# Rounding the weights in place, lagging the activation, and leaving the order of the elementwise engines to the scheduler

## The chip, the cores and the metric

The kernel runs on one core of a Trainium2 chip. The metric is the device time of one launch in microseconds. TensorE multiplies matrices, VectorE, ScalarE and GpSimd do the elementwise work, SyncE issues DMAs. In the profile they are PE (PEld for its weight loads), DVE, ACT, POOL and SP.

## What is computed

A gated linear attention over 4 batches, 8 heads, 768 tokens and a head size of 48, then a feed-forward block on the 3072 tokens of width 384, with 2048 hidden units. The inputs `q`, `k`, `v` and the logits are float32. The weights come in as float64 words and are rounded to float32 on the chip.

```python
def _attn_ref(q, k, v, f_logit):
    f = 1.0 / (1.0 + np.exp(-f_logit))
    for t in range(S):
        state = f[:, :, t, :, None] * state + np.einsum('bhd,bhe->bhde', k[:, :, t], v[:, :, t])
        y[:, :, t] = np.einsum('bhd,bhde->bhe', q[:, :, t], state)

def _moe_ref(x, w_in, w_out):
    h = x @ w_in
    sp = np.maximum(h, 0.0) + np.log1p(np.exp(-np.abs(h)))
    g = h * erf(sp)
    return (g @ w_out).astype(np.float32)
```

## The kernel before

**Tiling.** The tokens are cut into 24 chunks of 128 (index `g`), three of which make one of 8 blocks of 384. A chunk of attention goes through four stages: `stage_d` (cumulated logits `ps_d` on TensorE, two exponentials `dp` and `dm` on ScalarE, `qd` on VectorE, `kd` on GpSimd, and a small DMA `Tall`), `stage_t` (transposes, copies `qT` and `kT`), `stage_s` (scores `sc`, masked to `A` on VectorE; the state's update `dS`, `Sn`, `Mbd`) and `stage_y` (the output `y`, copied to `xT`). `prepare` and `prepare_log` (L264 to L274) make the logarithm `lt` for a whole block.

**Feed-forward.** `hidden` makes one group of 4 of the 16 hidden tiles: 12 matmuls of 384 columns, each shown as two MATMUL records in the trace, into a pair of PSUM banks `hps`, of which there are two; after every 6 the copy of L426 moves a pair to the group's buffer `Hg`. There are seven such buffers. `activate` then works on a group of 128 x 1536: Exp and Ln on ScalarE, four squares `x` on ScalarE (L150) each multiplied into `e` on VectorE (L155), Tanh (L394), and the last multiply (L396). `project` multiplies all 16 tiles of a block by `w_out_sb` for each of three token tiles (L445), copies the result (L453) and stores it.

**Order.** Everything stands in one hand-written order for all engines (`tc.manual_schedule()`): each engine runs its instructions as the program lists them. The loop over `it` walks through slots, one slot a matmul of `hidden` or `project`. Pass it=0 has 48 slots (`hidden` of block 0); passes 1 to 6 have 96 (three groups of block `it`, the projection of block `it`-1, then the fourth group); it=7 is similar, with the fourth group inside the projection; it=8 has the last projection. Between slots stand the attention stages of the next block (`at`), an `act_step` at each odd slot, and `prepare` of block it+2 in the middle. `act_step` advances one group at a time, in nine steps. A chain of three chunks stands ahead of it=0.

**Weights.** They come in 16 pieces (8 of `w_in`, 8 of `w_out`), loaded as raw words into `Hg` buffers that are not yet in use (`raw_buf`), by `next_piece` on SyncE. `round_piece` takes Abs (L234, ScalarE), max (L235, GpSimd), four operations on VectorE (L239, L243, L246, L249), and an add (L254: VectorE for `w_in`, GpSimd for `w_out`). The intermediate tile `w_t` comes from the two buffers of tag "x", which the activation's `x` uses too. `weights_step` ends the piece before and begins the next. A piece ends before the next load into its buffer, and `hidden` uses a buffer only after its last piece.

## Time and profile before

| what | us |
|---|---|
| median of 3 runs (lowest, highest) | 879.63 (877.65, 879.96) |
| the profiled execution: its time | 878.28 |
| its span, first to last instruction | 876.6 |
| TensorE, matmuls busy | 684.9 |
| ScalarE busy | 533.3 |
| VectorE busy | 504.7 |
| GpSimd busy | 146.5 |
| mean granted TensorE clock, as a share | 0.903 |

The page gives busy shares of each engine; the list of waits says which instruction an engine stood idle for; the timeline shows instructions in order of time with the idle time before each and what ended it. A table by stage sums the busy time in stretches of the span. A line number is that of the kernel before.

### The profile page before, as it was taken

What the parts mean: (1) busy time and instruction counts of PE and PEld (TensorE: products, weight loads), DVE (VectorE), ACT (ScalarE), POOL (GpSimd) and SP (SyncE); (2) the same over time, 40 slices, a digit from 0 to 9 for tenths busy, and PEclk for the clock granted to TensorE, in tenths of its full rate; (3) what the DMA queues carried; (4) which work ended last, traced back from release to release, by engine and by line L of the source; (5) the groups of instructions that cost most, each with busy time, mean ns of one, the idle gap of its engine ahead of it and who ended that gap; (6) DMA issues with size and microseconds to landing.
All of it is one profiled execution on the core that took longest, in us unless ns stands there. A gap on an engine that the chain in (4) does not pass through costs nothing.

```text
span 876.6 us, 9159 instructions
## 1 busy us (share of the span) xinstructions
PE 684.9 (78%) x3729; PEld 410.2 (47%) x3729; DVE 504.7 (58%) x429; ACT 533.3 (61%) x457; POOL 146.5 (17%) x95
## 2 busy tenths in 40 slices
PE   3756636376888987978698886978698879989696
PEld 2524423244555554644455553644455545545353
DVE  3968775577562884277552884266552875185440
ACT  5264634277975779178745779178744776389450
POOL 2433445501210130000310130000310010000000
PEclk9868868779899899999899998999899999989999
DMA  9913145200113001400033001400030000000000
GB/s 222 261 49 93 45 105 147 35 1 0 37 37 63 1 1 37 99 0 1 1 73 63 1 1 37 99 0 1 1 73 10 1 0 19 10 1 0 18 10 30
DMA packets 112176, 36.88 MB, mean 42 GB/s; under 512 B 103936, under 2 KB 107008, under 8 KB 112128
## 3 DMA queue, kind: packets, MB, share of 16 engines
q1 hardware_dynamic: 108672, 36.18, 17.2%
q8 instruction: 31, 0.51, 0.2%
q10 hardware_dynamic: 3456, 0.05, 0.2%
q14 instruction: 17, 0.14, 0.1%
HBM read 31.46 MB, written 4.72 MB: 41 GB/s over the span
## 4 chain that ended last, share of the span: by engine, by line
ACT 29%; DVE 26%; PE 26%; issue 12%; POOL 4%; DMA 1%; ACTq 0%; SPq 0%; DVEq 0%; POOLq 0%
DVE e L155 17%; PE ops L445 15%; PE hps L419 7%; ACT x L150 5%; ACT yl L381 4%; ACT e L379 4%; ACT L381 3%; ACT e L394 3%; POOL w_out_sb L254 2%; ACT dp L285 2%; ACT L285 1%; PE y L144 1%; DVE Hg L426 1%; POOL w_t L235 1%; DVE qd L293 1%
## 5 line engine op out<-in xcount | busy, mean ns | idle before, releaser
L419 PE MATMUL hps<-xT,w_in_sb 128*128 128x384 f32 x768 | 290.9, 531 | 71.5 <-DVE Hg L426 65.1
L155 DVE SCALAR_TENSOR_TENSOR e<-x,e 128x1536 f32<-128x1536 f32 x128 | 244.2, 1908 | 109.7 <-ACT x L150 103.6
L445 PE MATMUL ops<-w_out_sb,Hg 128*128 128x384 f32 x768 | 274.0, 512 | 0.6 <-ACT osb L453 0.6
L419 PEld LDWEIGHTS hps<-xT,w_in_sb 128*128 128x128 f32 x768 | 154.4, 207 | 189.4 <-DVE Hg L426 71.8
L150 ACT ACTIVATE x<-yl,serf_bias 128x1536 f32<-128x1536 f32 x128 | 199.4, 1573 | 62.6 <-DVE e L155 44.3
L445 PEld LDWEIGHTS ops<-w_out_sb,Hg 128*128 128x128 f32 x768 | 151.6, 201 | 106.1 <-issue 19.5
L426 DVE COPY Hg<-hps 128x768 f32<-128x768 f32 x64 | 60.8, 951 | 94.5 <-PE hps L419 94.3
L298 POOL TENSOR_TENSOR kd<-kn,dm 128x384 f32<-128x384 f32 x24 | 32.6, 1360 | 421.6 <-ACT dm L289 257.2
L379 ACT ACTIVATE e<-Hg 128x1536 f32<-128x1536 f32 x32 | 47.2, 1475 | 63.9 <-DVE Hg L426 62.7
L394 ACT ACTIVATE e<-e 128x1536 f32<-128x1536 f32 x32 | 47.4, 1483 | 54.8 <-DVE e L155 53.8
L396 DVE TENSOR_TENSOR Hg<-Hg,e 128x1536 f32<-128x1536 f32 x32 | 62.3, 1946 | 22.0 <-ACT e L394 21.9
L293 DVE TENSOR_TENSOR qd<-qn,dp 128x384 f32<-128x384 f32 x24 | 20.6, 859 | 87.9 <-ACT dp L285 87.4
L279 PE MATMUL ps_d<-lt,tri 128*128 128x384 f32 x48 | 25.4, 617 | 40.0 <-ACT lt L274 40.0
L311 PE MATMUL ps_t<-ident,kd 128*128 128x128 f32 x96 | 19.4, 339 | 42.0 <-DVE Sn L356 38.9
L144 PE MATMUL y<-A,vt 128*32 128x128 f32 x768 | 39.0, 295 | 16.4 <-DVE kT L316 15.1
L381 ACT ACTIVATE yl<-e 128x1536 f32<-128x1536 f32 x32 | 47.5, 1483 | 0.4
L359 POOL TENSOR_TENSOR Mbd<-Sn,Tall 48x192 f32<-48x192 f32 x32 | 30.3, 947 | 99.7 <-DVE Sn L356 98.5
L144 PEld LDWEIGHTS y<-A,vt 128*32 128x32 f32 x768 | 29.4, 115 | 29.7 <-DVE kT L316 17.1
L235 POOL TENSOR_SCALAR w_t<-w_t 128x768 f32<-128x768 f32 x16 | 37.3, 2332 | 26.8 <-ACT w_t L234 26.7
L381 ACT ACT_TABLE_LOAD x32 | 41.1, 1283 | 0.6
L370 ACT COPY xT<-y 128x384 f32<-128x384 f32 x24 | 11.3, 471 | 43.8 <-PE y L144 43.8
L234 ACT ACTIVATE w_t<-Hg 128x768 f32<-128x768 f32 x16 | 14.3, 903 | 35.9 <-POOL w_out_sb L254 28.6
(53 smaller groups left out, 496.2 us busy)
## 6 DMA issues: line engine op xcount, KB each, us to landing
Hg<-in_moe_w_in_dram SPq DMA_DIRECT2D x8, 768.0 KB, 6.7
Hg<-in_moe_w_out_dram SPq DMA_DIRECT2D x8, 768.0 KB, 4.4
lt<-in_f_logit_dram SPq DMA_DIRECT2D x24, 192.0 KB, 3.6
qn<-in_q_dram SPq DMA_DIRECT2D x24, 192.0 KB, 3.6
kn<-in_k_dram SPq DMA_DIRECT2D x24, 192.0 KB, 3.8
vt<-in_v_dram SPq DMA_DIRECT2D x24, 192.0 KB, 3.8
out_dram<-osb SPq DMA_DIRECT2D x24, 192.0 KB, 2.0
Tall<-dp ACTq DMA_DIRECT2D x24, 2.0 KB, 2.0
```

What stands on the lines that cost most here:

```text
L144: nc.tensor.matmul(y[M * i : M * (i + 1), kt, :], lhsT=terms[n][0], rhs=terms[n][1], start=(n == 0), stop=(n == len(terms) - 1), skip_grou ...
L150: nc.scalar.activation(out=dst[:], in_=y[:], func=AF.Square, bias=serf_bias[:, i : i + 1], scale=SERF_K)
L155: nc.vector.scalar_tensor_tensor(out=e[:], in0=x[:], scalar=SERF_AB[i][1], in1=e[:], op0=ALU.add, op1=ALU.mult)
L235: nc.gpsimd.tensor_scalar(out=x.bitcast(FP32), in0=x.bitcast(FP32), scalar1=TINY, scalar2=None, op0=ALU.max)
L298: nc.gpsimd.tensor_tensor(out=kds[g % 2][:, :, 0:D], in0=kns[g % NQ][:].rearrange("t (h d) -> t h d", d=D), in1=dm[:].rearrange("t (h d) - ...
L379: nc.scalar.activation(out=e[:], in_=h, func=AF.Exp)
L381: nc.scalar.activation(out=y[:], in_=e[:], func=AF.Ln, scale=SERF_C, bias=1.0)
L394: nc.scalar.activation(out=e[:], in_=e[:], func=AF.Tanh)
L396: nc.vector.tensor_tensor(out=h, in0=h, in1=e[:], op=ALU.mult)
L419: nc.tensor.matmul(hps[:, j, 0:TB], lhsT=w_in_sb[:, kt, ft * P : (ft + 1) * P], rhs=xTs[blk][:, kt, :], start=(kt == 0), stop=(kt == n_k - 1),
L426: nc.vector.tensor_copy(out=gr["h"][:, 2 * u : 2 * u + 2, :], in_=hps[:, :, 0:TB])
L445: nc.tensor.matmul(of[tt], lhsT=gr["h"][:, ft % FG, tt * P : (tt + 1) * P], rhs=w_out_sb[:, ft, :], start=(ft == 0), stop=(ft == n_ft - 1),)
```

## The change

Five things change. The fixed order holds for TensorE and SyncE alone; for VectorE, ScalarE and GpSimd the scheduler makes the order, and the program's order is its priority. `round_piece` works in place in `dst`, the weights' own tile, writes its mask into the raw words (`high`) in place of `z`, has four steps in place of two (three for the first three pieces, whose add stays on VectorE; all others add on GpSimd), and several pieces can be under way. `activate` has ten steps, and its multiplies stand two squares behind; up to two groups run, the next one starting after six steps of the one before; the squares have three buffers of their own. A step comes at every third slot in the passes 0 and 1, at every fourth from then on, at each slot of the last. `qd` and `dp` have one buffer in place of two. Block 1's logits are loaded and prepared ahead of it=0, the pieces' buffers are taken in another order, with five pieces loaded at the start, and the last roundings may fall in the first 12 slots of it=1.

```diff
@@ -161,6 +161,7 @@
+    xpool = main.enter_context(tc.tile_pool(name="xpool", bufs=3))
@@ -171,9 +172,9 @@
-    qds = [fixed(f"qd{i}", [P, H, DP], pool=fix) for i in range(2)]
+    qd = fixed("qd", [P, H, DP], pool=fix)
...
-    dps = [fixed(f"dp{i}", [P, 2, DP, HP], pool=fix) for i in range(2)]
+    dp = fixed("dp", [P, 2, DP, HP], pool=fix)
@@ -202,7 +203,8 @@
-    raw_buf = [0, 1, 2, 3, 4, 5, 6, 4, 5, 6, 4, 5, 6, 4, 5, 6]
+    FIRST_PIECES = 3
+    raw_buf = [0, 1, 2, 3, 4, 5, 6, 3, 4, 5, 6, 4, 5, 6, 4, 5]
@@ -224,38 +226,36 @@
-        words = raw.rearrange("p (n two) -> p n two", two=2)
-        low, high = words[:, :, 0], words[:, :, 1]
-        t = work.tile([P, 2, PIECE], U32, name="w_t", tag="x")
-        x, z = t[:, 0, :], t[:, 1, :]
-        nc.scalar.activation(out=x.bitcast(FP32), in_=high.bitcast(FP32), func=AF.Abs)
-        nc.gpsimd.tensor_scalar(
-            out=x.bitcast(FP32), in0=x.bitcast(FP32), scalar1=TINY, scalar2=None, op0=ALU.max
-        )
+        m = dst.shape[1]
+        words = raw.rearrange("p (a n two) -> p a n two", a=m, two=2)
+        low, high = words[:, :, :, 0], words[:, :, :, 1]
+        bits = dst.bitcast(U32)
+        nc.scalar.activation(out=dst, in_=high.bitcast(FP32), func=AF.Abs)
+        yield
+        nc.gpsimd.tensor_scalar(out=dst, in0=dst, scalar1=TINY, scalar2=None, op0=ALU.max)
...
-            out=x, in0=x, scalar1=0x07FFFFFF, scalar2=3,
+            out=bits, in0=bits, scalar1=0x07FFFFFF, scalar2=3,
...
-            out=x, in0=high, scalar=0xC0000000, in1=x, op0=ALU.bitwise_and, op1=ALU.bitwise_or
+            out=bits, in0=high, scalar=0xC0000000, in1=bits, op0=ALU.bitwise_and, op1=ALU.bitwise_or
...
-            out=z, in0=x, scalar1=0xFF800000, scalar2=None, op0=ALU.bitwise_and
+            out=high, in0=bits, scalar1=0xFF800000, scalar2=None, op0=ALU.bitwise_and
...
-            out=low.bitcast(FP32), in0=low, scalar=2.0**-52, in1=z.bitcast(FP32),
+            out=low.bitcast(FP32), in0=low, scalar=2.0**-52, in1=high.bitcast(FP32),
...
-        eng = nc.vector if i < n_pieces else nc.gpsimd
-        eng.tensor_tensor(
-            out=dst,
-            in0=low.bitcast(FP32).rearrange("p (a f) -> p a f", a=dst.shape[1]),
-            in1=x.bitcast(FP32).rearrange("p (a f) -> p a f", a=dst.shape[1]),
-            op=ALU.add,
+        if i >= FIRST_PIECES:
+            yield
+        (nc.vector if i < FIRST_PIECES else nc.gpsimd).tensor_tensor(
+            out=dst, in0=low.bitcast(FP32), in1=dst, op=ALU.add
@@ -279,7 +279,6 @@
-        dp = dps[g % 2]
@@ -291,7 +290,7 @@
-            out=qds[g % 2][:, :, 0:D].rearrange("t (a r) d -> t a r d", r=2),
+            out=qd[:, :, 0:D].rearrange("t (a r) d -> t a r d", r=2),
@@ -304,7 +303,7 @@
-        for src in (qds[g % 2], kds[g % 2]):
+        for src in (qd, kds[g % 2]):
@@ -374,33 +373,40 @@
+        yield
...
-        x = None
-        for i in range(len(SERF_AB)):
-            x_new = work.tile([P, FG * TB], FP32, name="x", tag="x")
-            squared(x_new, y, i)
-            if x is not None:
-                times(e, x, i - 1)
-            x = x_new
+        n = len(SERF_AB)
+        xs = {}
+        for i in range(n + 2):
+            if i < n:
+                xs[i] = xpool.tile([P, FG * TB], FP32, name="x", tag="x")
+                squared(xs[i], y, i)
+            if i >= 2:
+                times(e, xs.pop(i - 2), i - 2)
...
-        times(e, x, len(SERF_AB) - 1)
-        yield
-        yield
...
+    ACT_STEPS = len(SERF_AB) + 6
+    LEAD = len(SERF_AB) + 2
+    running = []
...
-        while acts:
-            if next(acts[0], "end") != "end":
-                return
-            acts.popleft()
...
+        if acts and (not running or running[-1][1] >= LEAD):
+            running.append([acts.popleft(), 0])
+        for r in list(running):
+            r[1] += 1
+            if next(r[0], "end") == "end":
+                running.remove(r)
@@ -408,7 +414,7 @@
-        assert all(j < ended[0] for j, x in enumerate(raw_buf) if x == n_made[0] % NG)
+        own = n_made[0] % NG
@@ -423,6 +429,7 @@
+                        assert all(i < ended[0] for i, x in enumerate(raw_buf) if x == own)
@@ -492,7 +499,7 @@
-    with tc.manual_schedule():
+    with tc.manual_schedule(engines={mybir.EngineType.PE, mybir.EngineType.SP}):
@@ -506,12 +513,12 @@
-        load(0)
-        next_piece()
-        load(1)
-        next_piece()
-        load(2)
-        next_piece(5)
+        for g in range(LOOK):
+            load(g)
+            next_piece()
+        for g in range(CPB, 2 * CPB):
+            load_f(g)
+        next_piece(2)
@@ -519,35 +526,34 @@
-        for t in dps:
-            nc.vector.memset(t[:, :, D:DP, :], 1.0)
-        for t in qds + kds:
+        nc.vector.memset(dp[:, :, D:DP, :], 1.0)
+        for t in [qd] + kds:
...
-        rounding = deque()
+        rounding = []
...
-        def weights_step():
...
-            if rounding:
-                next(rounding.popleft(), None)
-                ended[0] += 1
-                next_piece()
-            if begun[0] < 2 * n_pieces:
+        def weights_step(begin=True):
...
+            for r in list(rounding):
+                if next(r, "end") == "end":
+                    rounding.remove(r)
+                    ended[0] += 1
+            if begin and begun[0] in raws:
...
+            next_piece()
...
-                if loaded[0] < 2 * CPB:
-                    load_f(loaded[0])
@@ -558,18 +564,23 @@
+        load_to(LOOK)
+        next_piece()
...
+        load_to(LOOK + 1)
...
+        weights_step()
...
+        stage_y(1)
...
-        stage_y(1)
...
-        load_to(LOOK)
+        prepare(1, 0, CPB)
...
+        prepare_log(1, 0, CPB)
@@ -593,30 +604,25 @@
-            first = 12 if it == 0 else 2
+            first = 3
...
-                if it == 0 and s % (6 if s < 25 else 3) == 1 or (it, s) == (1, 1):
+                if it == 0 and s % (6 if s < 24 else 3) == 1 or it == 1 and s < 12:
...
-                if it == 0 and s in (0, 6):
-                    load_to(4 + s // 6)
-                    if s == 6:
-                        prepare(1, 0, CPB)
-                        prepare_log(1, 0, CPB)
+                if (it, s) == (0, 2):
+                    load_to(LOOK + 2)
...
-                if s % 2:
+                if s % (3 if it < 2 else 4) == 2 or it == n_blocks:
...
-            while it == n_blocks and acts:
-                act_step()
```

## Rows read from the trace of the kernel before

**Rows 1.** The page's part 1: busy us, share of the span, instructions of each engine

```profile
PE 684.9 (78%) x3729; PEld 410.2 (47%) x3729; DVE 504.7 (58%) x429; ACT 533.3 (61%) x457; POOL 146.5 (17%) x95
```

**Rows 2.** Table by stage: stretch, length, busy us (count) PE, PEld, DVE, ACT, POOL, clock, DMA, GB/s

```profile
0.00:39.50 39.50, 20.09 (x271) 14.38 (x271) 23.40 (x45) 16.24 (x21) 15.17 (x20) 0.91 0.99 247
39.50:146.90 107.40, 60.73 (x385) 37.42 (x385) 78.31 (x80) 52.49 (x51) 46.48 (x24) 0.78 0.33 86
146.90:181.80 34.90, 14.78 (x59) 7.99 (x59) 20.25 (x20) 14.69 (x12) 17.39 (x8) 0.70 0.26 56
181.80:271.00 89.20, 75.90 (x404) 45.41 (x405) 55.94 (x42) 64.68 (x54) 10.68 (x7) 0.89 0.16 34
271.00:666.10 395.10, 333.46 (x1865) 199.85 (x1864) 223.03 (x168) 258.55 (x220) 50.74 (x32) 0.94 0.13 28
666.10:758.00 91.90, 80.32 (x462) 48.66 (x461) 51.32 (x39) 58.38 (x48) 6.04 (x6) 0.94 0.02 7
758.00:838.10 80.10, 68.09 (x193) 38.41 (x192) 43.65 (x30) 59.70 (x43) 0.00 (x0) 0.94 0.02 5
```

**Rows 3.** List of waits: who waited for whom, total us, times, longest

```profile
DVE e L155 <- ACT x L150: 103.6, 31, 8.8
...
PE hps L419 <- DVE Hg L426: 65.1, 23, 10.9
...
PE ps_d L279 <- ACT lt L274: 40.0, 7, 10.7
PE ps_t L311 <- DVE Sn L356: 38.9, 9, 7.0
...
ACT w_t L234 <- POOL w_out_sb L254: 28.6, 5, 7.8
```

**Rows 4.** Timeline of VectorE, then TensorE, it=2: start, us, instruction, idle before

```profile
280.29 0.86 DVE L293 TENSOR_TENSOR qd<-qn,dp 128x384 f32<-128x384 f32 x1 [8.13 <-ACT dp L285]
...
283.56 0.94 DVE L426 COPY Hg<-hps 128x768 f32<-128x768 f32 x1
...
284.56 2.29 PE L419 MATMUL hps<-xT,w_in_sb 128*128 128x384 f32 x3 [3.22 <-DVE Hg L426]
```

**Rows 5.** Timeline of GpSimd, ScalarE and TensorE, second half of it=2

```profile
321.83 4.50 POOL L267 TENSOR_SCALAR lt<-lt 128x1152 f32<-128x1152 f32 x1
...
334.71 1.16 ACT L270 ACTIVATE lt<-lt 128x1152 f32<-128x1152 f32 x1
...
338.40 1.65 PE L279 MATMUL ps_d<-lt,tri 128*128 128x384 f32 x2 [5.44 <-ACT lt L274]
```

**Rows 6.** Timeline of VectorE, then GpSimd, while the last pieces are rounded

```profile
136.09 1.75 DVE L155 SCALAR_TENSOR_TENSOR e<-x,e 128x1536 f32<-128x1536 f32 x1
...
143.31 0.96 DVE L243 SCALAR_TENSOR_TENSOR w_t<-Hg,w_t 128x768 uint32<-128x768 uint32 x1
144.30 0.56 DVE L246 TENSOR_SCALAR w_t<-w_t 128x768 uint32<-128x768 uint32 x1
...
136.25 3.29 POOL L254 TENSOR_TENSOR w_out_sb<-Hg,w_t 128x768 f32<-128x768 f32 x1 [3.26 <-DVE Hg L249]
140.55 2.12 POOL L235 TENSOR_SCALAR w_t<-w_t 128x768 f32<-128x768 f32 x1 [1.01 <-ACT w_t L234]
145.93 1.84 POOL L254 TENSOR_TENSOR w_out_sb<-Hg,w_t 128x768 f32<-128x768 f32 x1 [3.26 <-DVE Hg L249]
...
170.46 3.28 POOL L254 TENSOR_TENSOR w_out_sb<-Hg,w_t 128x768 f32<-128x768 f32 x1 [3.26 <-DVE Hg L249]
```

**Rows 7.** Chain that ended last, end of it=2: start, us, what

```profile
361.03 7.75 PE hps L419 x24
```

**Rows 8.** Groups by line, ScalarE's table loads: count, busy us, mean ns, idle before

```profile
L381 ACT ACT_TABLE_LOAD x32 | 41.1, 1283 | 0.6
...
L379 ACT ACT_TABLE_LOAD x1 | 1.3, 1283 | 0.0
```

**Rows 9.** Groups by line, TensorE's matmuls of the projection

```profile
L445 PE MATMUL ops<-w_out_sb,Hg 128*128 128x384 f32 x768 | 274.0, 512 | 0.6 <-ACT osb L453 0.6
```

## The prediction

> **What bounds the kernel now.** I read the busy shares first. TensorE is the busiest engine at 78% of the span, ScalarE has 61% and VectorE 58%; none is full [rows 1]. So the span is made of waits, and the next view has to say where. The table by stage cuts the span at the first main matmul of each pass `it` of the block loop [rows 2]. Three regimes stand there. (a) From 39.5 to 271.0 us, the passes it=0 and it=1, TensorE is busy 151.4 of 231.5 us, at a clock of 0.70 to 0.89. (b) The four passes it=2 to 5 take 395.1 us together with 333.5 us of TensorE work at 0.94, so 61.6 us, 15.4 a pass, are idle. (c) it=6 and it=7 have 11.6 and 12.0 us idle. The last 38.5 us, the last projection from 838.1 on, I leave as they are.
>
> The list of waits names what TensorE waited for: 65.1 us on the copy `Hg` of L426, which frees the PSUM pair `hps`; 40.0 us on the logarithm `lt` of L274, of which 10.7 us are the start; 38.9 us on `Sn` of L356 [rows 3]. All but the start are short pieces of VectorE or ScalarE work, and neither engine is full in any stage. What delays a short piece is its place in its engine's queue. A case in a steady pass: the copy starts at 283.56 us in a queue whose head had kept VectorE idle for 8.13 us up to 280.29, and TensorE loses 3.22 us to it [rows 4]. Another: GpSimd had `lt` ready at 326.3 us, but ScalarE took its exponential only at 334.71, behind work of two groups, and TensorE waited 5.44 us [rows 5]. In the early regime a third thing comes on top. The rounding of the weights runs as one serial loop, Abs on ScalarE, max on GpSimd, four operations on VectorE, the add on GpSimd, and the next Abs only when the add is done, since `w_t` shares its two buffers with the activation's `x`. The adds at 136.25 and 170.46 us are four pieces apart, so 8.6 us a piece [rows 6]. The hidden groups of it=1 reuse the buffers of the last pieces, so their copies, and with them TensorE, hang on that loop: in 146.9 to 181.8 us TensorE is busy 14.8 of 34.9 us [rows 2].
>
> **The change, part by part.** The sum is made against the profiled execution: span 876.6 us, its time 878.28, which is 1.35 below the median of the runs shown.
>
> Queues ordered by the scheduler. I assume that it takes, of what its own plan holds ready, the earliest in the program, so that a queue no longer stands on a late piece while a ready one is behind it. The program's order is then a priority only. The waits of rows 4 and 5 are of the kind that this removes: a copy of 0.94 us [rows 4] stands behind one operation of about 1.75 us [rows 6], and the other PSUM pair covers it, since 6 slots (half a group) take 3.9 us of TensorE (24 matmuls, 12 slots, take 7.75 us [rows 7]). `lt` then has the whole first half of a pass to go through. I leave 3 us of the 15.4 idle for plans that the chip does not follow, bounds 0 and 15.4. That gains 4 x 12.4 = 49.6 us. For it=6 11.6 becomes 3, a gain of 8.6. The next bounds behind TensorE are ScalarE with 258.6 and VectorE with 223.0 us in the same 395.1 us [rows 2]; against the 345 us that are left that is 75% and 65%, high but not full. I take nothing for a better clock: TensorE's work stays 333.5 us at 0.94.
>
> Activation in lagged steps. The four squares and four multiplies of a group stay, 32 groups of the same instructions; a group may now start when the one before it has done six steps, and the third `x` buffer lets ScalarE run two squares ahead. The table loads can't grow by it: there are 81 (six lines; the first, with 32, and the last, with one, stand in [rows 8]), the 40 Ln need one in and one out each, and one is at the start, so today's order already pays for every change. The gain shows in it=7, where no attention is left and groups follow one another serially, with TensorE idle 12.0 us. ScalarE's 59.7 us there fit under TensorE's 68.1 [rows 2], so I take 71, a gain of 9.1.
>
> Rounding in place. The tile `w_t` goes, the piece is worked on in `w_in_sb` or `w_out_sb` itself, and so the waits on its buffer end: ScalarE's 28.6 us before Abs are the largest [rows 3]. Several pieces can be under way. What stays a limit is GpSimd: a piece takes 2.12 us for the max and 1.84 to 3.29 for the add [rows 6]. Pieces 3 to 7 move their add there: 5 x 0.96 = 4.8 us less on VectorE, by the like two-input L243 [rows 6], 5 x 1.84 to 3.29 = 9.2 to 16.5 us more on GpSimd, with `kd` and `Mbd`, for which the stages t and y wait, queued behind. GpSimd is busy 15.2 + 46.5 + 17.4 = 79.1 us up to 181.8 [rows 2]; with these it is about 92 us, which from its first max at 16.8 us on could end at 109 at the best. The operation of L246 now writes every other word: 0.56 us if that is free, 0.96 if it costs what L243, which reads every other word, takes [rows 6], so 0 to 6.4 us for 16 pieces on a VectorE that is busy 154 of 231 us there [rows 2]; I take it as hidden, and 6.4 on the path if VectorE were full. Per piece I take 7.5 us, between the 5.4 (2.12 + 3.29) of a GpSimd that is always fed and today's 8.6, nearer to today, since SyncE keeps its order and each reload waits for the piece in its buffer, with q, k and v behind it. Sixteen pieces from 16.8 us end at 137; today the last add ends at 173.7 [rows 6]. The gate of it=1 comes 37 us earlier. For that it=0 has to shrink from 107.4 to some 75 us; 60.7 us of it are TensorE's at 0.78, and `prepare(1)`, of the kind that TensorE waits for seven times [rows 3], now stands ahead of it. The rest of it=1, 89.2 us with 75.9 busy at 0.89, is at the clock of the later passes 75.9 x 0.89 / 0.94 = 71.9, and with 5 us of waits 77: a gain of 12. The early regime gives 49 us; bounds 20 (the rounding as serial as today, half of the other waits) and 75 (GpSimd nearly always fed).
>
> One buffer for `dp` and `qd`. A stage d now waits for the transposes of the chunk before and for the DMA `Tall`. Two or more stages lie between, so I take nothing; if that cover is gone, some 2 us for each of the three chunks of the start-up and three of it=0, 12 us at most.
>
> Loads. Five pieces instead of seven are queued at the start, and block 1's logits come ahead of pieces 3 and 4. The start-up to 39.5 us waits on its own chain, so I take 0; bounds -4 and +4, about one piece's VectorE work (0.56 + 0.96 + 0.56 + 0.96 us and an add) in or out of that chain.
>
> Sum: 49 + 49.6 + 8.6 + 9.1 = 116.3 us; span 760, time 762 us.
>
> **Rivals.** (1) The plan is made with other durations than the chip's, and queues keep their order when the chip is late. Then half of the gain of each regime stays: 878 - 58 = 820 us. For it: VectorE stood 103.6 us on the squares [rows 3], so it follows ScalarE closely. Against: the slots leave 3.9 us of cover for a copy. (2) The scheduler finds little to reorder, and only the freed `w_t` and the earlier logarithms act: 25 us, 853. Against: rows 4, where the queue was idle before its own late head. (3) On the other side: the lag. A step comes each fourth slot, a group takes ten steps, 40 slots, and a pass's last group can start at slot 96, so by the program it is done at slot 40 of the next pass, and the projection reads it from slot 48 on. The margin is 8 slots, 5.2 us. Today the projection waits only 0.6 us for anything [rows 9]. If the engines let these groups slip, each us beyond the margin is TensorE's, in every pass; from some 18 us of slip on (the 12.4 to be gained and the margin) the passes are slower than before. At 25 us of slip, 20 lost less 12.4 gained make seven passes 53 us longer, and the early regime may still give 20: 911. For it: ScalarE is at 75%. Against: a step's place is a priority, and an idle engine takes it earlier. (4) GpSimd's adds gate the early regime. The add at 136.25 us took 3.29 us beside an `e` of VectorE at 136.09, the one at 145.93, beside a copy out of PSUM, 1.84 [rows 6]. With a denser VectorE all 13 adds may be long ones: 13 x 1.45 = 19 us, 781. [...]
>
> **How the numbers follow.** Forecast (730 to 775) 0.43; rival 4 (775 to 800) 0.15; rival 1 (800 to 845) 0.20; rival 2 (845 to 880) 0.08, of which 0.03 is no change; rival 3 0.10; below 730, with nearly all gaps closed, 0.04. The likeliest is 762. To hold 0.8 the range reaches from 718 (61.6 + 11.6 + 12.0 + 75 us gained) to 845. A difference of 0.3%, about 2.6 us, is what a measurement can tell here. Faster 0.87, same 0.03, slower 0.10.
>
> **What would show it.** In the profile after: waits of `hps` on `Hg` below 20 us, of `ps_d` on `lt` near the start-up's 10.7; passes it=2 to 5 of 85 to 88 us; the last rounding add near 137 us; 81 table loads; L246 between 0.56 and 0.96 us; the add on GpSimd up to 3.3 us. The forecast is wrong if the projection waits for L396, if VectorE still stands on the squares for 100 us, or if the rounding ends after 160 us.

## Result and profile after

The changed kernel takes 746.49 us (median of 4 runs, 744.91 to 746.98); the kernel before, run beside it, takes 879.8. The ratio is 0.8477, with an interval of 0.8444 to 0.851. The profiled execution took 746.98 us with a span of 745.2 us; the mean granted clock is 0.957, after 0.903. The forecast was 762 in a range of 718 to 845. Ratios below are all to the kernel before, and are followed by their 95% interval.

Line numbers are those of the changed kernel: `hps` matmul L425, projection L452, copy `Hg` L433, last multiply L395, mask `A` L328, `Mbd` L351, transposes `ps_t` L310. In the rounding, Abs is L237, max L239, VectorE's four operations L241, L245, L248, L251, the add L257.

First the busy line of the page, the same line as in [rows 1]:

```profile
PE 651.8 (87%) x3729; PEld 398.0 (53%) x3729; DVE 500.5 (67%) x422; ACT 526.5 (71%) x457; POOL 151.7 (20%) x100
```

VectorE and ScalarE have as much to do as before within 7 us; TensorE has 33 us less for the same 3729 instructions, by the clock (0.957 after 0.903; last section). The other 98 us of the gain are idle time of TensorE that is gone. The table by stage, cut at the same matmuls as [rows 2] (stretch, length, busy us of PE, PEld, DVE, ACT, POOL with counts, clock, DMA share, GB/s):

```profile
0.00:44.70 44.70, 25.09 (x270) 17.86 (x270) 29.93 (x47) 20.60 (x26) 18.13 (x21) 1.00 0.91 224
44.70:115.60 70.90, 54.73 (x385) 33.77 (x385) 62.36 (x62) 45.27 (x45) 46.24 (x25) 0.90 0.41 104
115.60:150.90 35.30, 12.56 (x59) 7.00 (x59) 34.78 (x26) 21.66 (x18) 25.96 (x11) 0.72 0.38 101
150.90:221.20 70.30, 69.46 (x405) 42.10 (x405) 60.04 (x47) 59.27 (x51) 10.62 (x8) 0.97 0.19 41
221.20:558.20 337.00, 317.12 (x1864) 195.30 (x1865) 210.71 (x168) 255.22 (x220) 43.15 (x32) 0.97 0.16 33
558.20:636.30 78.10, 76.00 (x461) 46.50 (x460) 50.78 (x40) 57.30 (x48) 7.59 (x6) 1.00 0.03 8
636.30:706.70 70.40, 65.26 (x193) 37.46 (x192) 43.28 (x30) 58.82 (x43) 0.00 (x0) 0.95 0.02 6
706.70:745.20 38.50, 31.55 (x98) 18.05 (x96) 8.63 (x7) 8.36 (x9) 0.00 (x0) 0.96 0.06 23
```

Against [rows 2] the start-up is 5.2 us longer, it=0 and it=1 together are 176.5 us in place of 231.5, the passes it=2 to 5 take 337.0 in place of 395.1, it=6 78.1 in place of 91.9, it=7 70.4 in place of 80.1. One stretch still stands out: 115.6 to 150.9, where TensorE works 12.56 of 35.3 us, and VectorE is busy 34.78 of them. The list of waits (total us, times, longest) answers to [rows 3]:

```profile
DVE e L155 <- ACT x L150: 43.8, 17, 6.0
...
PE hps L425 <- DVE Hg L433: 30.6, 6, 12.5
...
PE ps_t L310 <- DVE Sn L355: 15.2, 5, 4.5
...
PE ps_d L279 <- ACT lt L274: 10.9, 1, 10.9
...
PE ps_t L310 <- DVE Mbd L351: 6.8, 2, 3.5
```

TensorE's wait on `Hg` fell from 65.1 to 30.6 us, and 26.2 of these are three waits in that one stretch. The wait on `lt` fell from 40.0 to the 10.9 of the start. What is left in the steady passes is of the kind that the next fence shows, the timeline of VectorE, then of TensorE, in it=3 (start, us, instruction, idle before it):

```profile
318.97 1.76 DVE L155 SCALAR_TENSOR_TENSOR e<-x,e 128x1536 f32<-128x1536 f32 x1 [4.07 <-ACT x L150]
320.65 1.22 DVE L328 TENSOR_TENSOR A<-sc,mask 128x1024 f32<-128x1024 f32 x1
321.78 0.73 DVE L351 TENSOR_TENSOR Mbd<-dS,Tall 48x192 f32<-48x192 f32 x2
...
313.45 0.56 PE L342 MATMUL dS<-vt,kd 128*48 128x48 f32 x16
...
322.66 0.66 PE L310 MATMUL ps_t<-ident,kd 128*128 128x128 f32 x2 [3.50 <-DVE Mbd L351]
```

The scores and `dS` are done at 314.0 us, so `A` and `Mbd` could run. But VectorE's queue has a multiply ahead of them whose square is not there yet; it stands for 4.07 us, and TensorE loses 3.50 us behind it. This is the picture of [rows 4] again, now in a queue that the scheduler ordered.

### The profile page after: what moved, and what is told of

It reads as the page before. It is cut to its first block, busy times and chain, and to the rows that moved or that the text cites. A ratio compares the mean times of both kernels' runs of the same rounds, so it can differ in the third digit from the quotient of the medians.

```text
span 745.2 us, 9155 instructions
## 1 busy us (share of the span) xinstructions
PE 651.8 (87%) x3729; PEld 398.0 (53%) x3729; DVE 500.5 (67%) x422; ACT 526.5 (71%) x457; POOL 151.7 (20%) x100
## 4 chain that ended last, share of the span: by engine, by line
ACT 38%; PE 27%; DVE 16%; issue 9%; DMA 4%; POOL 4%; SPq 2%; ACTq 0%; DVEq 0%; POOLq 0%
PE ops L452 16%; ACT x L150 13%; DVE e L155 7%; PE hps L425 5%; ACT yl L382 5%; ACT e L379 4%; ACT L382 3%; ACT e L393 3%; PE y L144 3%; POOL lt L267 2%; DMA lt<-in_f_logit_dram 2%; ACT L393 2%; DVE Hg L395 2%; ACT L379 2%; DVE Hg L433 2%
## 5 line engine op out<-in xcount | busy, mean ns | idle before, releaser
L425 PE MATMUL hps<-xT,w_in_sb 128*128 128x384 f32 x768 | 275.5, 512 | 32.5 <-DVE Hg L433 30.6
L452 PE MATMUL ops<-w_out_sb,Hg 128*128 128x384 f32 x768 | 259.2, 490 | 4.9 <-DVE Hg L433 3.9
L155 DVE SCALAR_TENSOR_TENSOR e<-x,e 128x1536 f32<-128x1536 f32 x128 | 230.1, 1800 | 48.3 <-ACT x L150 43.8
L425 PEld LDWEIGHTS hps<-xT,w_in_sb 128*128 128x128 f32 x768 | 150.6, 200 | 139.5 <-DVE Hg L433 31.4
L150 ACT ACTIVATE x<-yl,serf_bias 128x1536 f32<-128x1536 f32 x128 | 194.7, 1567 | 18.8 <-DVE e L155 16.4
L452 PEld LDWEIGHTS ops<-w_out_sb,Hg 128*128 128x128 f32 x768 | 142.6, 190 | 102.8 <-DVE Hg L433 6.6
L433 DVE COPY Hg<-hps 128x768 f32<-128x768 f32 x64 | 60.9, 953 | 85.8 <-PE hps L425 85.6
L395 DVE TENSOR_TENSOR Hg<-Hg,e 128x1536 f32<-128x1536 f32 x32 | 58.8, 1837 | 46.5 <-ACT e L393 46.4
L379 ACT ACTIVATE e<-Hg 128x1536 f32<-128x1536 f32 x32 | 47.3, 1479 | 31.6 <-DVE Hg L433 24.9
L292 DVE TENSOR_TENSOR qd<-qn,dp 128x384 f32<-128x384 f32 x24 | 29.1, 1213 | 28.7 <-ACT dp L284 28.7
L310 PE MATMUL ps_t<-ident,kd 128*128 128x128 f32 x96 | 18.9, 331 | 24.6 <-DVE Sn L355 15.2
L460 ACT COPY osb<-ops 128x384 f32<-128x384 f32 x24 | 11.2, 467 | 35.4 <-PE ops L452 35.4
L270 ACT ACTIVATE lt<-lt 128x1152 f32<-128x1152 f32 x8 | 9.3, 1163 | 34.5 <-POOL lt L267 34.5
L267 POOL TENSOR_SCALAR lt<-lt 128x1152 f32<-128x1152 f32 x6 | 18.9, 3150 | 68.2 <-DMA lt<-in_f_logit_dram 68.2
L323 PEld LDWEIGHTS sc<-qT,kT 48*128 48x128 f32 x384 | 25.1, 200 | 14.0 <-issue 12.5
```

The lines of the kernel that those rows point to most:

```text
L150: nc.scalar.activation(out=dst[:], in_=y[:], func=AF.Square, bias=serf_bias[:, i : i + 1], scale=SERF_K)
L155: nc.vector.scalar_tensor_tensor(out=e[:], in0=x[:], scalar=SERF_AB[i][1], in1=e[:], op0=ALU.add, op1=ALU.mult)
L267: (nc.gpsimd if blk > 1 else nc.vector).tensor_scalar(out=lt, in0=lt, scalar1=LOGIT_MIN, scalar2=None, op0=ALU.max)
L379: nc.scalar.activation(out=e[:], in_=h, func=AF.Exp)
L395: nc.vector.tensor_tensor(out=h, in0=h, in1=e[:], op=ALU.mult)
L425: nc.tensor.matmul(hps[:, j, 0:TB], lhsT=w_in_sb[:, kt, ft * P : (ft + 1) * P], rhs=xTs[blk][:, kt, :], start=(kt == 0), stop=(kt == n_k - 1),
```

## Experiments

The theory on record was that the scheduler's order carries the gain and the lagged activation little. The rivals: the lag carries it, in whatever order, or the rounding does. Two kernels undo or do the order alone, the next three the other parts. One table holds the median time of all that follow and the lengths of the passes in the profiled execution of each (us; cut at the first main matmul of each pass; `it2-5` is a mean; `it8` goes to the end of the span):

| kernel | time | ratio | start | it0 | it1 | it2-5 | it6 | it7 | it8 |
|---|---|---|---|---|---|---|---|---|---|
| before | 879.63 | 1 | 39.5 | 107.4 | 124.1 | 98.8 | 91.9 | 80.1 | 38.5 |
| after | 746.49 | 0.8477 | 44.7 | 70.9 | 105.6 | 84.3 | 78.1 | 70.4 | 38.5 |
| e1 | 731.09 | 0.83 | 48.8 | 80.5 | 107.5 | 77.1 | 75.8 | 63.3 | 46.1 |
| e2 | 787.73 | 0.8958 | 45.6 | 88.1 | 100.7 | 89.3 | 87.8 | 68.2 | 38.5 |
| e3 | 751.97 | 0.855 | 44.0 | 82.6 | 99.9 | 84.2 | 78.1 | 69.6 | 38.5 |
| e4 | 780.78 | 0.8862 | 44.3 | 74.6 | 107.1 | 90.7 | 80.2 | 71.0 | 38.8 |
| e5 | 733.72 | 0.8333 | 41.2 | 92.0 | 106.9 | 76.9 | 75.9 | 63.2 | 46.1 |
| e6 | 713.44 | 0.8098 | 44.4 | 70.6 | 105.6 | 76.9 | 75.8 | 63.2 | 44.4 |
| e7 | 738.67 | 0.8385 | 44.1 | 71.4 | 96.3 | 84.8 | 78.1 | 70.6 | 38.7 |
| e8 | 741.16 | 0.8428 | 44.5 | 69.1 | 102.6 | 83.6 | 78.1 | 70.3 | 38.8 |
| e9 | 769.67 | 0.8729 | 42.4 | 90.2 | 109.1 | 84.6 | 76.5 | 74.0 | 39.1 |
| e10 | 730.48 | 0.8292 | 39.4 | 89.8 | 110.0 | 77.5 | 75.5 | 63.2 | 40.1 |
| e11 | 712.44 | 0.8092 | 44.4 | 68.4 | 105.6 | 77.0 | 75.8 | 70.1 | 38.2 |
| e12 | 709.46 | 0.8055 | 44.0 | 71.4 | 101.1 | 77.0 | 75.8 | 69.1 | 38.2 |

**e1_fixed: the changed kernel, one written order for all engines.**

```diff
-    with tc.manual_schedule(engines={mybir.EngineType.PE, mybir.EngineType.SP}):
+    with tc.manual_schedule():
```

> The changed kernel with one hand-written order for all engines again, all else as changed. Theory (the scheduler's order of VectorE, ScalarE and GpSimd carries the gain of the passes it=2 to 7): these passes go back to 95 us or more each, the whole to 820 us or more. Rival (the lagged steps and the freed rounding carry it, and the written order would do as well): within 10 us of the changed kernel's 746.

Measured 731.09 us, 0.83 (0.8265 to 0.8335): 15 us faster than the change with the scheduler. The table by stage, it=0 and it=1, then it=2 to 5:

```profile
48.80:236.80 188.00, 144.53 (x847) 86.70 (x848) 158.36 (x132) 124.64 (x112) 86.03 (x41) 0.87 0.27 67
236.80:545.30 308.50, 307.91 (x1865) 190.95 (x1864) 213.04 (x167) 253.22 (x218) 50.68 (x32) 1.00 0.18 37
```

In the steady passes TensorE is busy 307.91 of 308.5 us, at a clock of 1.00. The scheduler is better only early: 188.0 us here, 176.5 with it, and 4.1 in the start-up. So the scheduler's order costs 28.5 us in it=2 to 5 and gives back 15.6 ahead of them; it costs 9.4 more in it=6 and it=7 and gives back 7.6 in it=8. The theory fell, and the written order did better than the rival had it, too.

**e2_before_sched: the kernel before, scheduler's order for the three engines, nothing else.**

```diff
-    with tc.manual_schedule():
+    with tc.manual_schedule(engines={mybir.EngineType.PE, mybir.EngineType.SP}):
```

> The kernel before with one edit: the written order holds for TensorE and SyncE alone. Theory: the passes it=2 to 5 come near 86 us, as in the changed kernel, and the rounding stays serial on its shared buffers, so about 60 to 75 us of the gain come: 805 to 820 us. Rival (the lagged program order is needed for it): 850 us or more.

Measured 787.73 us, 0.8958 (0.8927 to 0.8989). The order alone is worth 92 us on the kernel before, more than the 60 to 75 expected. So it gains much where the written order is that of the kernel before, and loses in the steady passes where the written order has the lag (e1). The steady passes stay at 89.3 us.

**e5_before_lag: the kernel before, with the lagged activation alone, in the written order.**

```diff
+    xpool = main.enter_context(tc.tile_pool(name="xpool", bufs=3))
...
-        t = work.tile([P, 2, PIECE], U32, name="w_t", tag="x")
+        t = xpool.tile([P, 2, PIECE], U32, name="w_t", tag="x")
...
         nc.scalar.activation(out=e[:], in_=h, func=AF.Exp)
+        yield
...
+        for i in range(n + 2):
+            if i < n:
+                xs[i] = xpool.tile([P, FG * TB], FP32, name="x", tag="x")
+                squared(xs[i], y, i)
+            if i >= 2:
+                times(e, xs.pop(i - 2), i - 2)
...
+        if acts and (not running or running[-1][1] >= LEAD):
+            running.append([acts.popleft(), 0])
...
-                if s % 2:
+                if s % (3 if it < 2 else 4) == 2 or it == n_blocks:
```

> The kernel before, all engines in the written order, with the lagged activation alone: ten steps, the multiply two squares behind, two groups under way, three buffers for the squares (the rounding's w_t takes one of the same three), a step at every third, then every fourth slot. New theory (the lag in the written order carries the later passes, the scheduler is only a substitute for it): passes 2 to 5 at 77 to 80 us, the start to the end of it=1 about as before, 255 to 275 us, the whole 750 to 775 us. Rival (it takes the earlier prepare and the new stage positions as well): passes of 85 us and more, above 790 us.

Measured 733.72 us, 0.8333 (0.8303 to 0.8363). The lag alone takes off 146 us, more than the whole change, and more than was expected even by the theory that gave it most. Of the span, 30.8 us come ahead of it=2, which starts at 240.2 in place of 271.0 us. There the rounding's `w_t` also draws on three buffers in place of two, as the edit shows, and what that is worth was not told apart. In it=8 e5 is 7.6 us slower. Its table by stage for it=2 to 5:

```profile
240.20:547.80 307.60, 307.60 (x1865) 191.03 (x1864) 215.33 (x167) 252.75 (x218) 52.40 (x32) 1.00 0.18 37
```

By the profile TensorE has no idle time in them. The spot that cost 3.50 us above, in the timeline of VectorE, then TensorE, of this kernel (`A` is L330 here, `Mbd` L353, `ps_t` L312):

```profile
325.56 1.23 DVE L330 TENSOR_TENSOR A<-sc,mask 128x1024 f32<-128x1024 f32 x1 [0.50 <-PE sc L325]
326.70 0.73 DVE L353 TENSOR_TENSOR Mbd<-dS,Tall 48x192 f32<-48x192 f32 x2
...
324.36 1.16 PE L325 MATMUL sc<-qT,kT 48*128 48x128 f32 x16
...
331.00 0.60 PE L312 MATMUL ps_t<-ident,kd 128*128 128x128 f32 x4
```

`A` runs as soon as the scores are there, and the transposes start without a wait: the written order has no late multiply ahead of `A`. Here VectorE waits for squares 1.1 us in all:

```profile
DVE e L155 <- ACT x L150: 1.1, 1, 1.1
```

The four corners: written order before 880, scheduler's order before 788, written order with the lag 734 (e5) or, with the change's other parts, 731 (e1), scheduler's order with all of it 746. No run has the scheduler's order with the lag and nothing else; the nearest is e3, with 752. The two gains do not add up: either of them removes most of what the other would, and the lag removes more.

**e3_oldround: the changed kernel with the old rounding** (through `w_t`, taken from the three `x` buffers, all `w_in` adds on VectorE).

```diff
-        bits = dst.bitcast(U32)
-        nc.scalar.activation(out=dst, in_=high.bitcast(FP32), func=AF.Abs)
-        yield
-        nc.gpsimd.tensor_scalar(out=dst, in0=dst, scalar1=TINY, scalar2=None, op0=ALU.max)
+        t = xpool.tile([P, 2, PIECE], U32, name="w_t", tag="x")
...
+        eng = nc.vector if i < n_pieces else nc.gpsimd
```

> The changed kernel with the rounding of the kernel before: the tile w_t, from the three buffers of the squares, two steps a piece, the add of w_in on VectorE. Theory (the shared buffer made the rounding serial): only the stretch up to the end of it=1 grows, by 20 to 40 us, the later passes stay at 84 us: 766 to 786 us. Rival (with the scheduler's order the buffer no longer matters): below 753 us.

Measured 751.97 us, 0.855 (0.8519 to 0.8581): rounding in place is worth 5.5 us, not the 20 to 40 of the theory. The last add ends at 154.6 us here, at 153.6 in the changed kernel. But `w_t` has three buffers to draw on here, and two in the kernel before; what the third is worth was not tried.

**e4_oldact: the changed kernel with the old `activate` and `act_step`, a step at each odd slot.**

```diff
-            if i >= 2:
-                times(e, xs.pop(i - 2), i - 2)
+            if x is not None:
+                times(e, x, i - 1)
+            x = x_new
...
+        while acts:
+            if next(acts[0], "end") != "end":
+                return
+            acts.popleft()
...
-                if s % (3 if it < 2 else 4) == 2 or it == n_blocks:
+                if s % 2:
                     act_step()
```

> The changed kernel with the activation of the kernel before: one group at a time, nine steps, a step at every odd slot, the multiply one square behind. Theory (a step's place is only a priority for the scheduler, so it makes up for most of it; the serial groups show in it=7 alone): 750 to 758 us. Rival (the lag is what lets two groups overlap): 775 us or more, with every pass longer.

Measured 780.78 us, 0.8862 (0.8818 to 0.8905); the lag is worth 34 us in the changed kernel, as the rival had it. The passes it=2 to 5:

```profile
226.00:588.90 362.90, 324.28 (x1865) 197.16 (x1864) 211.59 (x168) 255.01 (x220) 42.49 (x32) 0.93 0.14 30
```

The scheduler is the same, the operations are the same, and a pass is 90.7 us in place of 84.3. So how the program cuts, spaces and overlaps the steps still counts, though the scheduler orders the queues. In it=7 it hardly counts: 71.0 us without the lag, 70.4 with it.

**e6_hybrid: the changed kernel, scheduler's order up to the end of it=1, written order from it=2 on.** If the scheduler is better early and worse later, this should have both.

```diff
         for it in range(n_blocks + 1):
+            if it == 2:
+                ms[0].__exit__(None, None, None)
+                ms[0] = tc.manual_schedule()
+                ms[0].__enter__()
```

> The changed kernel, with the scheduler's order up to the end of it=1 and the written order of all engines from it=2 on. Theory (the scheduler helps the irregular start and costs 7 us in each regular pass): the start as in the changed kernel, 221 us, and from there on as in the run with the written order, 494 us: 712 to 720 us. Rival (the two orders do not add up, since the scheduler leaves groups of it=0 and it=1 behind): above 728 us.

Measured 713.44 us, 0.8098 (0.807 to 0.8126). The two stretches:

```profile
44.40:220.60 176.20, 136.16 (x847) 82.57 (x847) 157.08 (x133) 126.28 (x113) 81.59 (x42) 0.89 0.33 80
220.60:528.40 307.80, 307.80 (x1865) 191.18 (x1866) 210.19 (x165) 251.78 (x217) 50.73 (x32) 1.00 0.17 35
```

The first is that of the changed kernel (176.5), the second that of e5 (307.6).

**e7_less_dve and e8_less_pool: what limits the gate of it=1.** In 115.6 to 150.9 us both VectorE (34.78) and GpSimd (25.96) are loaded. e7 leaves out two of VectorE's operations for the last eight pieces, e8 leaves out GpSimd's max for them.

```diff
+        if i < n_pieces:          # e7
             nc.vector.tensor_scalar(
                 out=bits, in0=bits, scalar1=0x07FFFFFF, scalar2=3,
...
+        if i < n_pieces:          # e8
             nc.gpsimd.tensor_scalar(out=dst, in0=dst, scalar1=TINY, scalar2=None, op0=ALU.max)
```

> The changed kernel without two of the four VectorE operations on the pieces 8 to 15 (the mask of the exponent and the joining of the sign, which leaves w_out wrong), some 8 x 2.2 us of VectorE work less. Theory (VectorE is what is full ahead of the gate of it=1, 34.8 of 35.3 us): 8 to 18 us less than the changed kernel, 728 to 738 us. Rival (GpSimd is the limit, as the prediction had it): within 4 us of 746.

> The changed kernel without the max on GpSimd for the pieces 8 to 15 (which leaves tiny weights unrounded), 8 x 2.8 us of GpSimd work less. Prediction's theory (GpSimd is the limit of the rounding): 10 to 22 us less, 724 to 736 us. [...]

Measured 738.67 us for e7, 0.8385 (0.8358 to 0.8413), 7.8 us less than the changed kernel and just short of the 8 to 18 expected. e8 took 741.16, 0.8428 (0.8396 to 0.8459); its interval touches that of the changed kernel, and its 5.3 us less fall short of the 10 to 22 that GpSimd as the limit would have given. The gate stretch of e7, then that of e8, from the tables by stage:

```profile
115.40:142.10 26.70, 10.71 (x59) 6.14 (x59) 22.86 (x16) 15.48 (x14) 20.72 (x10) 0.79 0.42 103
```

```profile
113.60:145.10 31.50, 12.60 (x59) 7.05 (x59) 31.50 (x26) 20.21 (x17) 15.92 (x8) 0.76 0.43 113
```

Without two of VectorE's operations the stretch is 8.6 us shorter. Without GpSimd's max it is 3.8 us shorter, and VectorE is busy in all 31.50 of its 31.50 us, while GpSimd has 10 us less. So GpSimd's time alone is not the limit, against what the prediction had. But each edit also shortens the rounding of a piece, so the two can't tell a full VectorE from the length of that chain; e12 below comes nearer to it.

**e9_lag_serial and e10_lag_one: which part of the lag.** Both start from e5. e9 runs one group at a time, a step at every second slot; e10 keeps overlap and pace, and multiplies one square behind in place of two.

```diff
-    LEAD = len(SERF_AB) + 2
+    LEAD = ACT_STEPS                                              # e9
-                if s % (3 if it < 2 else 4) == 2 or it == n_blocks:
+                if s % 2 == 0 or it == n_blocks:                  # e9
...
-        for i in range(n + 2):
+        for i in range(n + 1):                                    # e10
...
-            if i >= 2:
-                times(e, xs.pop(i - 2), i - 2)
+            if i >= 1:
+                times(e, xs.pop(i - 1), i - 1)                    # e10
```

> The run with the lag alone, with one group at a time again: a group starts when the one before has done all ten steps, a step at each second slot so that four groups still fit a pass. Theory (two groups side by side at an even, slow pace are what keeps late pieces off the head of the queues): passes 2 to 5 at 86 to 98 us, 780 to 840 us. Rival (the multiplies two squares behind are enough): below 750 us.

> The run with the lag alone, with the multiplies one square behind in place of two (nine steps). Theory (the pace does it: a step of four slots, 2.6 us, covers a square of 1.6 us): passes 2 to 5 below 79 us, 728 to 745 us. Rival (the second square of distance is what VectorE's queue needs): passes of 83 us and more, above 760 us.

e9 took 769.67 us, 0.8729 (0.869 to 0.8768), which lies between the two expectations and bears out neither: overlap and the slower pace are worth 36 of e5's 146 us, and 110 are already there without them, at a step per two slots as before. Those come with what e9 keeps, Exp and Ln in separate steps, a multiply two squares behind, and three buffers for `x` and `w_t`; these were not tried one by one. e10 took 730.48 us, 0.8292 (0.8261 to 0.8323), which can't be told from e5: with overlap and pace, the second square of distance is not needed. One row of e9's list of waits is a lesson of its own:

```profile
DVE e L155 <- ACT x L150: 99.5, 33, 6.7
```

VectorE waits for the squares as long as it did before [rows 3], in a kernel that is 110 us faster. That total says nothing of what TensorE loses.

**e11_hybrid_tail and e12_hybrid_copies: towards a faster kernel.** e11 is e6 with a step at every third slot of it=7 too, so that less activation is left for the end. e12 is e11 with the copies `Hg` of block 0 and of the first two groups of block 1 moved from VectorE to ScalarE, since VectorE is full at the gate.

```diff
-                if s % (3 if it < 2 else 4) == 2 or it == n_blocks:
+                if s % (3 if it < 2 or it == n_blocks - 1 else 4) == 2 or it == n_blocks:   # e11
...
-                        nc.vector.tensor_copy(
+                        (nc.scalar.copy if blk == 0 or (blk == 1 and gi < 2) else nc.vector.tensor_copy)(   # e12
```

> The run with both orders, with a step at every third slot in it=7 too. Theory (the wait of 4.2 us of the last projection on L395 comes from groups that the slow pace leaves for it=8): it=8 goes from 37.8 to 32 or 33 us, 707 to 710 us. Rival (ScalarE is the bound at the end): 712 us or more.

> The run before this one, with the copies of the hidden pairs of it=0 and of the first two groups of it=1 on ScalarE in place of VectorE, 12 x 0.95 us less on VectorE. Theory (VectorE is full ahead of the gate of it=1): 4 to 10 us less than the run before it, 698 to 705 us. Rival (the rounding's own chain is the gate): within 2 us of it.

e11 took 712.44 us, 0.8092 (0.8061 to 0.8123), not to be told from e6's 713.44 and not the 707 to 710 of the theory: it=8 went from 44.4 to 38.2 us, and it=7 from 63.2 to 70.1, where TensorE now waits behind ScalarE (4.08 us at 652.66, for the copy `osb`). The gain was given back one pass earlier. e12 took 709.46 us (709.28 to 710.64; e11 beside it 711.98 to 714.49), 0.8055 (0.8025 to 0.8084). Its gate stretch:

```profile
115.40:147.00 31.60, 10.40 (x58) 6.15 (x58) 28.86 (x22) 16.89 (x16) 26.30 (x10) 0.71 0.40 106
```

VectorE's share fell to 28.86 of 31.6 us, and 3 us came of it, less than the 4 to 10 expected and little more than the rival's 2. What a full VectorE costs shows at the last copy of it=0. In the changed kernel, TensorE, then VectorE:

```profile
103.89 8.21 PE L425 MATMUL hps<-xT,w_in_sb 128*128 128x384 f32 x24
...
129.60 0.94 DVE L433 COPY Hg<-hps 128x768 f32<-128x768 f32 x1
```

The matmuls end at 112.10 us, the copy comes 17.5 us later, and one of TensorE's three waits in the stretch, 10.28 us, hangs on it. In e12 ScalarE makes this copy at 118.41. Yet the gate opens at 147.0 us in e12 and at 148.0 in e11. It opens when the piece before the last is rounded: in the changed kernel its add on GpSimd runs from 145.38 to 147.87 us, and the copy into its buffer follows at 149.87, behind L395 and L248 on VectorE. From the end of its max at 134.18 its four VectorE operations take until the add at 145.38, between other work and some of them long beside GpSimd: L241 took 2.20 us and L248 3.48, against medians of 0.55 for both (last section). So the rounding's chain through both engines is what ends last; a full VectorE lengthens it, and is not the whole of it. e12 is faster than both kernels, 37 us below the changed one.

## Why the prediction was right, and where it was not

The sum was -116.3 us on a span of 876.6; it was -131.4. The sign and the size came out, the reason for the largest terms did not.

- **Steady passes, -49.6 foreseen, -58.1 measured.** Two errors partly cancel. I took TensorE's work as 333.5 us at a clock of 0.94 and 12 us idle; it was 317.1 us at 0.97 and 19.9 idle. "I take nothing for a better clock" was 16.4 us off: the same work takes less time in the runs that pause less (317.1 us here, 324.3 in e4), and e5, where TensorE never pauses in them, does the same work in 307.6 us at 1.00. The idle time was 7.9 us above my figure, which was for "plans that the chip does not follow"; row 318.97 above shows such a place. For it=6, 8.6 foreseen, 13.8 came, by the same clock (76.0 us of work at 1.00 where [rows 2] has 80.3 at 0.94).
- **The step that failed is who does it.** I assigned the steady gain to the scheduler and said that the program's order "is then a priority only". e1 and e5 show that the written order with the lag gets all of it and 28 to 29 us more; e4 shows that under the scheduler the program's steps still move a pass by 6.4 us. And a queue that the scheduler ordered can still stand on a late piece: at 318.97 us a multiply waited for its square with ready work behind it.
- **The lag, -9.1 foreseen, in it=7 alone.** it=7 gained 9.7 us and took 70.4 against my 71, but that is luck. Without the lag the changed kernel's it=7 takes 71.0 (e4), and the scheduler's order alone brings the kernel before from 80.1 to 68.2 (e2); so this gain comes with the order. The lag's worth lies where I put nothing: 34 us in the changed kernel, 25.9 of them in it=2 to 5 (e4), and 146 in the written order (e5). In [rows 4] VectorE's queue stood for 8.13 us on `dp`; I took that for a fault of the fixed order as such. It was the way the activation's steps stand in it, as ScalarE's timeline of the kernel before shows for that moment, with TensorE's `ps_d`, which `dp` reads, below (start, us, instruction, idle before):

```profile
272.20 1.48 ACT L379 ACTIVATE e<-Hg 128x1536 f32<-128x1536 f32 x1 [8.25 <-DVE Hg L426]
273.70 1.28 ACT L381 ACT_TABLE_LOAD   x1
274.99 1.48 ACT L381 ACTIVATE yl<-e 128x1536 f32<-128x1536 f32 x1
276.51 1.58 ACT L150 ACTIVATE x<-yl,serf_bias 128x1536 f32<-128x1536 f32 x1
278.10 1.28 ACT L285 ACT_TABLE_LOAD   x1
279.40 0.86 ACT L285 ACTIVATE dp<-ps_d 128x384 f32<-128x384 f32 x1
...
272.94 0.81 PE L279 MATMUL ps_d<-lt,tri 128*128 128x384 f32 x2
```

ScalarE had stood idle for 8.25 us, then Exp, Ln and a square came in one run of 5.9 us, and `dp` behind them, 5.65 us after `ps_d` was there. The same place in e5, in the written order too (its Exp is L381, Ln L384):

```profile
242.82 1.47 ACT L381 ACTIVATE e<-Hg 128x1536 f32<-128x1536 f32 x1
244.19 0.84 ACT L286 ACTIVATE dp<-ps_d 128x384 f32<-128x384 f32 x1
...
246.86 1.48 ACT L384 ACTIVATE yl<-e 128x1536 f32<-128x1536 f32 x1
...
242.10 0.81 PE L280 MATMUL ps_d<-lt,tri 128*128 128x384 f32 x2
```

Here `dp` goes between Exp and Ln, 1.28 us after `ps_d`. The lag splits the first step, spaces the rest and lets two groups overlap. The pace is the smaller part: a step at each second slot asks for a square per 1.29 us of TensorE (two of the slots of [rows 7]), and one takes 1.58 us, but e9 keeps that pace with one group at a time and gives only 36 of the 146 us back. In e9 `dp` comes 3.1 us after `ps_d` at this place, behind four squares, and TensorE loses 0.40 us at the next copy in place of 3.22 [rows 4]. So the fences show what the split does in e5; that it makes most of the other 110 us is not shown.

- **Early regime, -49 foreseen, -55.0 measured for it=0 and it=1.** The start-up took 5.2 us more, where I had taken 0 within 4. One more weights step and `prepare(1)` stand ahead of it=0, and the written order of e1 is slow there too (48.8 us); but e2, the old program under the scheduler, takes 45.6, so what costs it stays open. The gate of it=1 moved from 181.8 to 150.9, by 30.9 in place of 37: it=0 and the gate stretch are 36.1 us shorter, and the start-up takes 5.2 back. The rest of it=1 went from 89.2 to 70.3, by 18.9 in place of 12: TensorE works 69.5 us at 0.97 where I put 71.9 at 0.94, and waits 0.8 where I put 5. Nor is this gain the rounding's alone: the order by itself takes 42.7 us off it=0 and it=1 (e2), the lag with its three buffers 32.5 (e5).
- **Rounding.** I put the last add at 137 us, at 7.5 us a piece for GpSimd; it ended at 153.6, and GpSimd's time alone is not what limits (e8), the chain through VectorE and GpSimd is (e12). I had taken the longer L246 as hidden because VectorE was busy 154 of 231 us; now it is busy 157 of 176.5, and nearly all of the gate stretch. Rounding in place, which I took for the cause of the early gain, is worth 5.5 us (e3).
- **L248, once L246:** within my bounds of 0.56 and 0.96 us by the medians. The eight pieces of `w_out` take 0.55 us, the eight of `w_in` 0.95, as the rows of the last section show; one took 3.48 beside GpSimd.
- **Signs named.** Table loads 81, the wait on `lt` 10.9 us and the add on GpSimd up to 2.49 us, as foreseen. The wait of `hps` on `Hg` is 30.6 us in place of less than 20, nearly all of it at the gate; the passes take 84.3 us, just under the 85 to 88.
- **Rivals.** Rival 1 (queues that keep a late plan) is at work, but its 820 us were not reached, not even without the lag (e2, 788). Rival 2 (little to reorder) is contradicted by e2. Rival 3 (the projection waits for slipped groups) did not come: the projection waited 4.9 us in all, 0.4 of them for the last multiply L395, after 0.6 [rows 9]. Rival 4 (13 adds at 3.29) did not come either: the 13 adds took 1.85 to 2.49 us, while the max took up to 3.63, and on VectorE L248 up to 3.48 beside a median of 0.55.

What stays open: which of the separate Exp and Ln, the distance and the buffers makes e9's 110 us, and why the start-up is longer.

## What to carry to other kernels

Before an order is left to a scheduler, look whether an engine's queue stands on one late piece, and what stands ahead of that piece on the engine that makes it. Here splitting, spacing and overlapping the activation's steps gave more than the reordering (146 against 92 us), and the two gains overlap. In the steady passes the written order then left TensorE no wait to remove, and the scheduler's plan made some; in the early ones the scheduler's plan was the better of those tried. So each can be used where it measures better (e6). Cost a part by undoing or doing it alone, and by what TensorE loses, not by the waits of the engine that the part touches. And check a term that came out by such a run too: it=7 came out for another reason than the one given.

## What the runs showed of the hardware

**Granted clock.** In e5 and e6, whose TensorE ran without a gap in it=2 to 5, these passes show a clock of 1.00, and the same work takes 307.6 to 307.8 us in place of 333.5 at 0.94 [rows 2]. In stretches of 0.5 us the clock reads 1.00 or 0.50 nearly everywhere (1385 and 311 of 1752 in the kernel before, 1353 and 118 of 1490 in the changed one); 0.94 is a mean over both. In the kernel before, a record of L419 takes 486 ns from 360 to 369 us, at 1.00, and 847 ns in the median from 285 to 290 us, at 0.50. Closing gaps paid twice there: 61.6 us of idle time, and 26 us of faster work. Between the two, by idle time and by time of work, lie the changed kernel (19.9 us idle, 317.1 of work) and e4 (38.6 and 324.3). It is no rule for every stretch: the start-up of the changed kernel shows 1.00 too, with TensorE busy 25.09 of 44.70 us, and no run here tells why.

**VectorE beside GpSimd.** In the gate stretch some operations of VectorE that run beside one of GpSimd take longer than elsewhere. From the timeline of the changed kernel, VectorE, then GpSimd:

```profile
140.48 3.48 DVE L248 TENSOR_SCALAR Hg<-w_out_sb 128x768 uint32<-128x768 uint32 x1
...
146.08 3.40 DVE L395 TENSOR_TENSOR Hg<-Hg,e 128x1536 f32<-128x1536 f32 x1
...
149.41 0.55 DVE L248 TENSOR_SCALAR Hg<-w_out_sb 128x768 uint32<-128x768 uint32 x1
...
140.24 3.31 POOL L267 TENSOR_SCALAR lt<-lt 128x1152 f32<-128x1152 f32 x1
...
145.38 2.49 POOL L257 TENSOR_TENSOR w_out_sb<-Hg,w_out_sb 128x768 f32<-128x768 f32 x1 [1.83 <-DVE Hg L251]
```

L248, 0.55 us in the median, starts 0.24 us after GpSimd's L267 and ends 0.41 us after it, 3.48 us in all; L395, 1.76 us in the median, starts inside the add and ends 1.61 us after it, 3.40 us in all. So VectorE's 34.78 busy us in that stretch hold 4.6 us that these two rows have beyond their medians. No run here isolates the cause.

**Shape of a masked write.** The same operation on the same number of words (source view L248: least, median and longest ns, first and last start):

```profile
L248 DVE TENSOR_SCALAR Hg<-w_in_sb x8: 933/949/954, 18.8 to 84.3; 128x768 uint32<-128x768 uint32 x8
L248 DVE TENSOR_SCALAR Hg<-w_out_sb x8: 544/552/3483, 96.1 to 149.4; 128x768 uint32<-128x768 uint32 x8
```

A `w_in` piece is three rows of 256, a `w_out` piece two of 384; the write goes to every other word in both. The medians are 0.95 us for the first and 0.55 us for the second. L241, in place on the same tiles, has medians of 0.98 and 0.55 us, and took as little as 0.68 us on the three rows. No run here isolates what makes the difference.
